# Fifteen small loads behind the last load of a weight stream, and a wait for each at the end

## The chip, the cores and the metric

One core of a Trainium2 chip runs the whole program. The metric is the device time of one execution in microseconds (us). A ratio is the mean time of one kernel's runs over the mean of the other's runs of the same rounds; it is therefore not quite the ratio of the medians quoted beside it. Its 95% interval is given in brackets. The span of a profile, from the first to the last instruction, is about 1.2 us shorter than the timed execution.

## The reference, cut to what matters

The reference is one decode step of a transformer block with modulation: attention of one token over a window of 1024 cached keys and values, then a gated feed-forward layer. Only its end matters here:

```
x = x + gb * ((gelu(h @ w_gate) * (h @ w_up)) @ w_down)     # w_down: 1536 x 640, bf16
return x                                                    # 2 x 1 x 640, bf16
```

## The kernel before

All large loads are issued on the SyncE queue (SP), in the order in which they are needed: `w_mod`, `wq`, the key and value tiles, `wo`, `w_gate`, `w_up`, and `w_down` in four pieces of 3, 5, 3 and 1 rows per partition. The kernel records its operations in a list; `S.dma` records a load with its own semaphore, a counter that instructions can wait for, and a finished load adds 16 to it: in the traces each DMA engine that carries a share of it sends its own update when it is done (here called an increment). SP, DVE, ACT and PE are the program's names for SyncE, VectorE, ScalarE and TensorE. The output's store is the last DMA on the same queue, and SP's last act is to wait for it.

```
WD_SPLIT = [(9, 3), (0, 5), (5, 3), (8, 1)]
...
wd_src = B_w_down.rearrange("(p r) n -> p (r n)", r=FC)
for ci, (r0, nr) in enumerate(WD_SPLIT):
    dst, src = wd_v[:, r0:r0 + nr, :].rearrange("p r n -> p (r n)"), wd_src[:, r0 * D:(r0 + nr) * D]
    S.dma("sp", k_dma(dst, src), sem_wd[ci], writes=[("wd", ci)], deps=r3_dead, name="ld_wd%d" % ci)
... (feed-forward layer; the matmuls "down" wait for one piece of w_down each)
S.op("dve", ... outR)                       # finb = gb * y + X
S.dma("sp", k_dma(out[:, 0, :].rearrange("b (i n) -> i b n", i=NR), finb[0:P:RB, :]),
      sem_out, reads=["finb"], name="st_out")
S.resolve()
S.emit("sp", nc.sync, tail=lambda e: e.wait_ge(sem_out, 16))
```

## Time and profile before

| | before |
|---|---|
| time, median of the first 3 runs | 188.83 us |
| span of the profile | 187.6 us |
| packets on SP's DMA queue | 6492, 76.88 MB |
| the last piece of `w_down` has landed (its 16th semaphore increment, in the trace) | 184.75 us |
| the output's store is issued | 185.87 us |
| the output has landed | 187.58 us |

The kernel is bound by its stream of loads. From the page of the kernel before, the busy tenths of the DMA engines in 40 slices of the span, SP's DMA queue (packets, MB, share of 16 engines' span) and the chain of work that ended last, by engine:

```profile
DMA  7999998999999999999999999999999999999991
...
q1 hardware_dynamic: 6492, 76.88, 97.1%
...
DMA 71%; DVE 15%; PE 7%; ACT 2%; SPq 2%; issue 1%
```

The DMA engines are nearly always busy until the last slice. Whatever is added costs time only if it delays this stream, or lengthens the short chain from the stream's end to the output's landing. That chain is in the timeline of the kernel before (start us, duration us, engine, line, operation, output<-input; in brackets how long the engine was idle and what released it):

```profile
184.79 0.10 PEld L684 LDWEIGHTS ps<-r,aT 128*17 128x17 bf16 x4 [0.20 <-DMA r<-in_B_w_down_dram]
185.16 0.33 DVE L689 TENSOR_TENSOR fin<-ps,modR 128x160 f32<-128x160 f32 x1 [2.75 <-PE ps L684]
185.52 0.32 DVE L691 TENSOR_TENSOR finb<-fin,X 128x160 bf16<-128x160 f32 x1
185.87 0.69 SPq L266 DMA_DIRECT2D out_dram<-finb  x1
```

The last four matmuls wait for the last piece, two DVE operations follow, and the store is issued 1.1 us after the piece has landed. The end is the store's own way, some 1.7 us. The timeline of SP in the kernel before (line 266 is the helper that issues every DMA) shows how much room SP has there:

```profile
150.35 0.43 SPq L266 DMA_DIRECT2D r<-in_B_w_gate_dram  x1
150.83 0.91 SPq L266 DMA_DIRECT2D r<-in_B_w_up_dram  x2
151.78 10.69 SPq L266 DMA_DIRECT2D r<-in_B_w_down_dram  x4
185.87 0.69 SPq L266 DMA_DIRECT2D out_dram<-finb  x1
```

An issue takes 0.43 us, but the four of `w_down` took 10.69 us together: the trace gives 0.43, 0.43, 2.02 and 7.68 us. SP was held up there; I take it that the queue had no room, which the trace doesn't say. SP then did nothing for 23.4 us, until the result was there. SP's waits, as the trace's list of waits gives them for the stretch from 150 us on (who waited for whom: us in total, times, longest):

```profile
SPq L266 <- DVE finb L691: 23.4, 1, 23.4
SPq L697 <- DMA out_dram<-finb: 1.0, 1, 1.0
```

### The profile page before, as it was taken

Reading aid. Unit: us, or ns where it says so; the run is one execution under the profiler, and the core shown is the slowest. Engines: PE = TensorE matmul, PEld = TensorE weight load, DVE = VectorE, ACT = ScalarE, POOL = GpSimd, SP = SyncE. Lnnn points to the kernel's source line nnn. Section 1 sums busy time; section 2 is a strip of 40 time slices with the busy share of each in tenths; the row PEclk is TensorE's granted clock in tenths of the full one; section 3 lists DMA queues with packets and bytes.
Section 4 is the critical chain, followed back from the end, with each engine's and each line's share of the span. In section 5 each row is a group of like instructions: output and inputs, shape, how many; then the busy total and the mean of one; then the engine's idle time right before and its main releaser. Section 6 shows DMA issues by size and latency. Waiting matters only on the chain.

```text
span 187.6 us, 2409 instructions
## 1 busy us (share of the span) xinstructions
PE 107.5 (57%) x1039; PEld 51.1 (27%) x1039; DVE 98.2 (52%) x147; ACT 29.9 (16%) x72; POOL 5.1 (3%) x23
## 2 busy tenths in 40 slices
PE   0014730742968887676676655675497395364462
PEld 0011200210323443333423323233253152353121
DVE  6131100019588988886595695775865933003211
ACT  3041100082001221112011110210120103103400
POOL 8200000000000000000000000000000000000000
PEclk9999999997587999999879999999969967569696
DMA  7999998999999999999999999999999999999991
GB/s 254 402 451 435 430 459 372 422 435 424 430 422 422 427 425 426 427 424 420 419 432 432 422 423 422 421 438 422 424 423 422 419 488 428 416 384 442 398 396 45
DMA packets 6518, 77.03 MB, mean 411 GB/s; under 512 B 746, under 2 KB 876, under 8 KB 1516
## 3 DMA queue, kind: packets, MB, share of 16 engines
q1 hardware_dynamic: 6492, 76.88, 97.1%
q8 instruction: 8, 0.13, 0.3%
q10 hardware_dynamic: 16, 0.01, 0.0%
q14 instruction: 2, 0.02, 0.0%
HBM read 76.88 MB, written 0.00 MB: 410 GB/s over the span
## 4 chain that ended last, share of the span: by engine, by line
DMA 71%; DVE 15%; PE 7%; ACT 2%; SPq 2%; issue 1%
DMA ring<-in_A_k_cache_dram 37%; DMA ring<-in_A_wq_dram 17%; DMA r<-in_B_w_down_dram 17%; DVE prod L490 9%; PE ps L502 4%; DVE S_sb L509 4%; PE ps L467 2%; SPq L266 2%; ACT qbc L483 2%; DVE ps L485 1%; DVE M L512 1%; ACT qrow L474 1%; PE ps L526 0%; DVE bcR L519 0%; PE ps L684 0%
## 5 line engine op out<-in xcount | busy, mean ns | idle before, releaser
L490 DVE TENSOR_TENSOR prod<-ring,qbc 128x3072 bf16<-128x3072 bf16 x32 | 55.9, 1751 | 14.3 <-DMA ring<-in_A_k_cache_dram 14.3
L502 PE MATMUL ps<-prod,ident_b 128*128 128x512 bf16 x192 | 52.9, 419 | 14.4 <-DVE prod L490 14.4
L502 PEld LDWEIGHTS ps<-prod,ident_b 128*128 128x128 bf16 x192 | 17.5, 104 | 40.2 <-DVE prod L490 17.5
L509 DVE TENSOR_REDUCE S_sb<-ps 128x32 f32<-128x1024 f32 x16 | 19.3, 1206 | 2.1 <-PE ps L502 2.1
L526 PE MATMUL ps<-bcR,bcL 5*128 5x4 f32 x32 | 6.1, 258 | 21.9 <-DVE bcR L519 21.9
L563 ACT ACTIVATE On<-ps,rden 128x384 bf16<-128x384 f32 x16 | 9.3, 580 | 43.5 <-DVE rden L561 21.1
L551 PE MATMUL ps<-ring,E_sb 128*8 128x384 bf16 x256 | 15.5, 369 | 0.0
L534 ACT ACTIVATE E_sb<-Sb_sb 128x128 bf16<-128x128 f32 x16 | 5.0, 310 | 56.4 <-DVE Sb_sb L531 56.4
L467 PE MATMUL ps<-ring,hT 128*2 128x512 bf16 x60 | 6.7, 626 | 9.8 <-DMA ring<-in_A_wq_dram 8.8
L526 PEld LDWEIGHTS ps<-bcR,bcL 5*128 5x128 f32 x32 | 4.7, 183 | 26.1 <-DVE bcR L519 26.1
L477 DVE CAST qrow<-ps 128x512 bf16<-128x512 f32 x1 | 0.7, 692 | 15.7 <-PE ps L467 15.7
L622 PE MATMUL ps<-ring,oT 128*17 128x160 bf16 x192 | 5.5, 294 | 5.6 <-DMA ring<-in_A_wo_dram 5.6
L531 DVE TENSOR_TENSOR Sb_sb<-S_sb,ps 128x128 f32<-128x128 f32 x16 | 4.6, 287 | 7.6 <-PE ps L526 7.6
L540 PEld LDWEIGHTS ps<-denp,maskc 128*128 128x128 f32 x32 | 7.1, 224 | 3.7 <-ACT E_sb L534 0.9
L641 DVE TENSOR_TENSOR lnt<-ps,modR 128x160 f32<-128x160 f32 x1 | 0.3, 325 | 12.6 <-PE ps L622 12.6
L445 PE MATMUL ps<-r,scT 128*17 128x480 bf16 x40 | 4.3, 597 | 3.9 <-DMA r<-in_w_mod_dram 3.9
L622 PEld LDWEIGHTS ps<-ring,oT 128*17 128x17 bf16 x192 | 4.9, 117 | 6.2 <-DMA ring<-in_A_wo_dram 6.2
L551 PEld LDWEIGHTS ps<-ring,E_sb 128*8 128x8 bf16 x256 | 5.1, 90 | 3.7 <-issue 1.2
L396 PE MATMUL ps<-st,selstat 128*128 128x2 f32 x4 | 0.9, 298 | 8.6 <-ACT sqj L392 8.6
L467 PEld LDWEIGHTS ps<-ring,hT 128*2 128x2 bf16 x60 | 1.7, 114 | 14.7 <-DMA ring<-in_A_wq_dram 9.7
L576 PE MATMUL ps<-On,zsel 128*128 128x96 bf16 x64 | 5.2, 241 | 0.7 <-ACT On L563 0.7
L540 PE MATMUL ps<-denp,maskc 128*128 128x1 f32 x32 | 5.1, 230 | 0.8 <-ACT E_sb L534 0.8
(81 smaller groups left out, 71.2 us busy)
## 6 DMA issues: line engine op xcount, KB each, us to landing
ring<-in_A_k_cache_dram SPq DMA_DIRECT2D x16, 1536.0 KB, 24.4
ring<-in_A_v_cache_dram SPq DMA_DIRECT2D x16, 1536.0 KB, 24.2
r<-in_w_mod_dram SPq DMA_DIRECT2D x1, 4800.0 KB, 14.3
ring<-in_A_wq_dram SPq DMA_DIRECT2D x1, 4608.0 KB, 32.3
ring<-in_A_wo_dram SPq DMA_DIRECT2D x1, 4480.0 KB, 23.4
ring<-in_A_wq_dram SPq DMA_DIRECT2D x1, 3072.0 KB, 21.2
ring<-in_A_wo_dram SPq DMA_DIRECT2D x1, 2720.0 KB, 24.1
r<-in_B_w_gate_dram SPq DMA_DIRECT2D x1, 1920.0 KB, 25.0
```

The source lines that it names most:

```text
L467: last = e.matmul(ps[32 * i:32 * i + B, n, :], lhsT=hT[:, k, :], rhs=wv[:, kk, i, n * QW:(n + 1) * QW], start=(k == 0), stop=(k == KT - 1) ...
L490: S.op("dve", lambda e: e.tensor_tensor(out=prod[:, 2 * (g % 2) + ci, :, :], in0=ring[:, sl, ci * JC * Dh:(ci + 1) * JC * Dh].rearrange("p ...
L502: last = e.matmul(o_ap, lhsT=ident_b[:, :], rhs=prod[:, pz, :, t * GC:(t + 1) * GC], start=(t == 0), stop=(t == NCH - 1))
L509: S.op("dve", lambda e: e.tensor_reduce(out=S_sb[:, z, :], in_=ps[:, 2 * z:2 * z + 2, :].rearrange("p k (j c) -> p (k j) c", c=GC), axis=A ...
L526: S.op("pe", lambda e: e.matmul(ps[:, BK_T, P:P + HQ], lhsT=bcL[:, :], rhs=bcR[:, z, :], start=True, stop=True), reads=[("bcR", z), "bcL"] ...
L531: S.op("dve", lambda e: e.tensor_tensor(out=Sb_sb[:, z, :, :], in0=S_sb[:, z, :].unsqueeze(2).broadcast_to([P, J, HQ]), in1=ps[:, BK_T, P: ...
L534: S.op("act", lambda e: e.activation(out=E_sb[:, z, :, :], in_=Sb_sb[:, z, :, :], func=ACTF.Exp, scale=SCALE, accum_out=denp[:, z:z + 1]), ...
L540: S.op("pe", lambda e: e.matmul(ps[:, BK_T, P + 16:P + 17], lhsT=maskc[:, :], rhs=denp[:, z:z + 1], start=True, stop=True), reads=[("denp" ...
L551: last = e.matmul(ps[32 * i:32 * i + 2 * HQ, BK_O, 0:ON], lhsT=E_sb[:, z, 2 * jp:2 * jp + 2, :].rearrange("p j h -> p (j h)"), rhs=ring[:, ...
L563: S.op("act", lambda e: e.activation(out=On[:, quad % 2, b, :], in_=ps[:, BK_O, 0:ON], func=ACTF.Identity, scale=rden[:, z:z + 1]), reads= ...
L576: last = e.matmul(ps[:, BK_OT, 0:B * NT].rearrange("p (b t) -> p b t", b=B), lhsT=zsel[:, jj, x:x + P], rhs=On[:, quad % 2, :, jj * Dh + d ...
L622: last = e.matmul(ps[32 * i:32 * i + RM, BK_M, 0:DR], lhsT=oT[:, t, :], rhs=wv[:, tl, i, :], start=(t == 0), stop=(t == NT - 1), tile_posi ...
```

## The change

It is a probe. Fifteen loads, of 1 to 15 rows with a different row length each so that their packets can be told apart in a trace, are put behind the last piece of the stream, and SP also waits for all of them at the end. Nothing uses the data. This is the whole diff, with its unchanged lines cut:

```diff
@@ -261,6 +261,8 @@
         sem_out = S.sem("d_out")
+        sem_probe = {k: S.sem("d_probe%d" % k) for k in range(1, 16)}
+        probe = sb("probe", [16, 15, 272], BF16)
@@ -637,6 +639,10 @@
             S.dma("sp", k_dma(dst, src), sem_wd[ci], writes=[("wd", ci)], deps=r3_dead, name="ld_wd%d" % ci)
 
+        for k in range(1, 16):
+            w = 32 + 16 * k
+            S.dma("sp", k_dma(probe[0:k, k - 1, 0:w], B_w_down[0:2 * k, :].rearrange("(p r) n -> p (r n)", r=2)[:, 0:w]), sem_probe[k],
+                  writes=[("probe", k)], name="ld_probe%d" % k)
@@ -694,7 +700,7 @@
-        S.emit("sp", nc.sync, tail=lambda e: e.wait_ge(sem_out, 16))
+        S.emit("sp", nc.sync, tail=lambda e: [e.wait_ge(s, 16) for s in [sem_out] + list(sem_probe.values())])
```

## The prediction

> **What bounds the kernel now.** The stream of loads: in the page's slices the DMA engines are 90% or more busy nearly to the end, at about 425 GB/s, and the chain of waits gives DMA 71% of the span (187.6 us; 188.83 timed). The end, from the timeline: the last piece of w_down, issued at 154.79 us, lands at about 184.75; four matmuls and two DVE operations end at 185.84; the output's store is issued on SP at 185.87 (0.69 us), its packets move at 187.15 to 187.25, and SP's final wait ends at 187.6. The 16 engines finish the last piece at different times, 182.9 to 184.75.
>
> **What the change adds.** It removes nothing. 15 loads (k rows of 64+32k bytes, 47 KB in all) enter SP's queue behind that last piece and ahead of the store, and 15 semaphore waits follow the final wait.
>
> 1. DMA time. In the trace a store row of 320 bytes takes 20 to 32 ns, a load row of 1280 bytes 55, a semaphore packet 9, with gaps of 6 to 40. The Trainium skill, "DMA: Bandwidth & Descriptors", section "Why a DMA increments its semaphore by 16 and not by 1", says that a DMA uses the largest number of engines up to 16 that divides the slowest dimension, the lowest-numbered ones. The trace agrees: the store (2 by 4 rows) left 8 data and 4 semaphore packets, the load of c 2 and 2. So load k uses k engines, one row each; the first engine gets 15 rows and 15 semaphore packets, about 0.6 us (estimate: 15 x (22+9+10 ns)). The queue's packets rise from 6492 by 240 to 6732. They stand behind the last piece, so don't delay it, and have moved by about 185 us, 2 us before the store's. No cost.
>
> 2. SP's issue. An issue costs 0.33 to 0.69 us, 15 cost 7 to 10; SP is free from 162.47 to 185.87 (23.4 us in the wait list). But the queue is nearly full: the last two loads' issues took 2.02 and 7.68 us, with about 8 loads of 9 packets per engine outstanding. If room is given by packets, the 30 small ones on the first engine fit in by about 180 us (estimate: 40 packets drained since 162.5): no cost. If by loads, whatever their size, the last six wait for the stream's end and the store goes 2 to 3 us late. I hold the first at 80%.
>
> 3. The tail. 15 more waits on SP, already satisfied, after the output has landed. One takes 17 ns, and SP's instructions follow each other after 40 to 60: 15 x 17 to 75 ns = 0.3 to 1.1 us, most likely 0.6 (estimate), in full on the critical path.
>
> **Prediction.** 188.83 + 0.6 = 189.4 us; with one chance in five of a late store, the range is 188.8 to 191.0. Chances: faster by over 2% 0.01, within 2% 0.94, slower by over 2% 0.05.
>
> **What would show each step.** The last piece lands again near 184.7 us; 6732 packets; the fifteenth small load's issue ends before 182 us, and the store is issued within 0.3 us of 185.9; 15 instructions after the output's landing take 0.3 to 1.1 us.
>
> **What would make it wrong.** Room counted by loads (store late); a stall at each small load's semaphore packet (none shows between loads now: 6 ns); small packets far over 55 ns on the first engines, which also carry the store; final waits far over 75 ns.

## The result and the profile after

| | before | after |
|---|---|---|
| time, median of 4 runs | 188.91 us | 189.09 us |
| ratio | 1 | 1.0008 [0.9995, 1.0021] |
| last piece of `w_down` landed | 184.75 us | 184.99 us |
| small loads: the last issue ends / the last increment lands | – | 175.74 / 186.75 us |
| store issued | 185.87 us | 186.12 us |
| output landed | 187.58 us | 187.85 us |
| last wait ends | 187.62 us | 187.87 us |

The time is the same within the interval. The profiled run of the changed kernel is 0.25 us longer, but that lies ahead of everything that was added: its issue of `w_gate`, before the first small load, is already 0.19 us later (150.54 against 150.35). From the last piece's landing to the end of the last wait, before took 2.87 us and after 2.88. Nothing was added there.

The lines of the page of the changed kernel that answer to those of before:

```profile
DMA  7999998999999999999999999999999999999991
...
q1 hardware_dynamic: 6732, 76.93, 97.1%
...
DMA 71%; DVE 16%; PE 6%; SPq 2%; ACT 2%; issue 1%
```

The queue has exactly 240 packets more, as predicted: 120 rows and 120 semaphore packets. In the trace the row lengths count out one by one: one packet of 96 bytes, two of 128, and so on to fifteen of 544. The end of the timeline of the changed kernel is the same chain as before (line numbers have moved by 2 to 6):

```profile
185.03 0.10 PEld L690 LDWEIGHTS ps<-r,aT 128*17 128x17 bf16 x4 [0.18 <-DMA r<-in_B_w_down_dram]
185.40 0.33 DVE L695 TENSOR_TENSOR fin<-ps,modR 128x160 f32<-128x160 f32 x1 [2.83 <-PE ps L690]
185.76 0.33 DVE L697 TENSOR_TENSOR finb<-fin,X 128x160 bf16<-128x160 f32 x1
186.12 0.67 SPq L268 DMA_DIRECT2D out_dram<-finb  x1
```

SP's timeline and SP's waits in the changed kernel show the fifteen issues, and that SP still waits 10.4 of its former 23.4 us for the result:

```profile
151.96 10.70 SPq L268 DMA_DIRECT2D r<-in_B_w_down_dram  x4
162.70 13.04 SPq L268 DMA_DIRECT2D probe<-in_B_w_down_dram  x15
186.12 0.67 SPq L268 DMA_DIRECT2D out_dram<-finb  x1
```

```profile
SPq L268 <- DVE finb L697: 10.4, 1, 10.4
SPq L703 <- DMA out_dram<-finb: 0.6, 1, 0.6
```

Two things in the trace were not as I had expected them.

First, the final waits. The program names the output's semaphore first. The compiled program has eight wait instructions, each for two semaphores, and they begin in the middle of the list and work outwards. The output's wait, at one end of the list, came last. These are SP's records in the trace of the changed kernel; semaphore 121 is the output's, 122 to 136 are the small loads':

```
start us   ns   waits for
186.840    28   129, 128
186.914    28   130, 127
186.987    28   131, 126
187.046    28   132, 125
187.108    28   133, 124
187.167    28   134, 123
187.228    28   135, 122
187.288   583   136, 121 (output)
```

The output's last increment is at 187.85 us. Seven of the eight waits ran while the output was still on its way.

Second, the small loads took far longer to land than to move. Their last packet of data begins at 184.61 us, but the last semaphore increment lands at 186.75 us. The increments of successive small loads come one after another. The trace doesn't name the engine of an increment, but the first engine's can be picked out from the load of one row, which has only one: 183.16, 183.34, 183.52, 183.70, 183.88, 184.07, 184.24 us for loads 1 to 7, that is one every 0.18 us. The latest increments of loads 6 to 15 run from 184.94 to 186.75 us, 0.20 us apart; by their times they belong to one engine, whose first small load was load 6. It isn't the engine that ended the stream last: its first of these increments, at 184.94, comes ahead of the last piece's last one at 184.99. The data packets of the same loads on that engine begin 20 to 29 ns apart, from 184.26 to 184.48 us. So its increment for load 15 landed 2.2 us after its semaphore packet had begun (184.50 us). So the small loads ended 1.1 us before the output landed, not the 2 us that I had counted with, and with more of them that could run out.

### The profile page after: what moved, and what is told of

Read it like the earlier page. It is cut to its first block, busy times and chain, and to the rows that moved or that the text cites. A ratio compares the mean times of both kernels' runs of the same rounds, so it can differ in the third digit from the quotient of the medians.

```text
span 187.9 us, 2430 instructions
## 1 busy us (share of the span) xinstructions
PE 105.6 (56%) x1038; PEld 51.3 (27%) x1039; DVE 98.1 (52%) x147; ACT 29.9 (16%) x72; POOL 5.1 (3%) x23
## 3 DMA queue, kind: packets, MB, share of 16 engines
q1 hardware_dynamic: 6732, 76.93, 97.1%
## 4 chain that ended last, share of the span: by engine, by line
DMA 71%; DVE 16%; PE 6%; SPq 2%; ACT 2%; issue 1%
DMA ring<-in_A_k_cache_dram 37%; DMA ring<-in_A_wq_dram 17%; DMA r<-in_B_w_down_dram 17%; DVE prod L492 10%; DVE S_sb L511 4%; PE ps L469 3%; PE ps L504 3%; SPq L268 2%; ACT qbc L485 2%; DVE ps L487 1%; DVE M L514 1%; PE ps L528 0%; PE ps L690 0%; DVE bcR L521 0%; DVE Sb_sb L533 0%
## 5 line engine op out<-in xcount | busy, mean ns | idle before, releaser
L504 PE MATMUL ps<-prod,ident_b 128*128 128x512 bf16 x192 | 50.5, 405 | 14.2 <-DVE prod L492 14.2
L553 PE MATMUL ps<-ring,E_sb 128*8 128x384 bf16 x256 | 14.8, 356 | 0.0
L624 PE MATMUL ps<-ring,oT 128*17 128x160 bf16 x192 | 6.4, 325 | 7.2 <-DMA ring<-in_A_wo_dram 7.2
L624 PEld LDWEIGHTS ps<-ring,oT 128*17 128x17 bf16 x192 | 5.8, 131 | 7.6 <-DMA ring<-in_A_wo_dram 7.6
L542 PEld LDWEIGHTS ps<-denp,maskc 128*128 128x128 f32 x32 | 6.6, 208 | 3.5 <-ACT E_sb L536 0.9
L578 PE MATMUL ps<-On,zsel 128*128 128x96 bf16 x64 | 4.6, 223 | 0.7 <-ACT On L565 0.7
```

Of the source, the lines that this page charges most:

```text
L504: last = e.matmul(o_ap, lhsT=ident_b[:, :], rhs=prod[:, pz, :, t * GC:(t + 1) * GC], start=(t == 0), stop=(t == NCH - 1))
L542: S.op("pe", lambda e: e.matmul(ps[:, BK_T, P + 16:P + 17], lhsT=maskc[:, :], rhs=denp[:, z:z + 1], start=True, stop=True), reads=[("denp" ...
L553: last = e.matmul(ps[32 * i:32 * i + 2 * HQ, BK_O, 0:ON], lhsT=E_sb[:, z, 2 * jp:2 * jp + 2, :].rearrange("p j h -> p (j h)"), rhs=ring[:, ...
L578: last = e.matmul(ps[:, BK_OT, 0:B * NT].rearrange("p (b t) -> p b t", b=B), lhsT=zsel[:, jj, x:x + P], rhs=On[:, quad % 2, :, jj * Dh + d ...
L624: last = e.matmul(ps[32 * i:32 * i + RM, BK_M, 0:DR], lhsT=oT[:, t, :], rhs=wv[:, tl, i, :], start=(t == 0), stop=(t == NT - 1), tile_posi ...
```

## The experiments

The theory is that the change is free for three reasons. SP's issues fit in its idle time. The loads stand behind the last piece, so they delay no data that anybody waits for. And both the small loads' increments and the waits for them end before the output has landed. The rivals are that it costs about 0.16 us, the difference of the medians; that it would be free wherever it stood; or, as I had predicted, that only the packets' 20 to 30 ns matter and not an increment every 0.18 us. (The 0.16 us is the figure put on record; the medians of the table above differ by 0.18.) All runs below gave correct results. Four kernels (the change again, the output's wait moved, the twenty-four loads, and the fifteen ahead of the last piece) ran on one chip with one set of runs of the kernel before; the two with one load and the one with 128 rows ran on another with theirs; the twelve loads ran on a third with their own.

### The change again

The kernel is unaltered.

> The changed kernel unaltered, as a control on this chip. Theory A (everything that was added ends before the output has landed): ratio to the kernel before 1.000 to 1.001; the 15 small loads are issued on SP between about 162.7 and 176 us; on one engine their semaphore increments land about 0.18 us apart; the last of them lands near 186.7 us, about 1 us before the output's last increment. Rival B (the change costs 0.16 us, as the medians of the first runs differ): ratio 1.001 with an interval that leaves out 1.

Measured: 189.06 us against 188.93, ratio 1.0005 [0.9992, 1.0018]. The small loads are issued from 162.33 to 176.10 us, the first engine's increments are 0.18 us apart, the last lands at 186.68 us, and the output at 188.06 us. Rival B's 0.16 us is not confirmed, as the interval has 1 in it, nor is it excluded. All five kernels here whose additions end before the output lands (the change twice, and three below) have ratios from 1.0005 to 1.0009. Each interval includes 1, but all five lie on one side, so some 0.1 us may be real. It isn't in the tail, where after the output's last increment both kernels end within 0.04 us, and one load shows it as much as fifteen. One candidate is that the last piece itself comes a little later: from the third piece's last increment to the last piece's it is 0.42 to 0.45 us in all seven kernels with loads behind the last piece, and 0.38 us in the one profile of the kernel before. One profile can't show that, so this stays open.

### The output's wait moved to the middle of the list

```diff
-        sem_out = S.sem("d_out")
-        sem_probe = {k: S.sem("d_probe%d" % k) for k in range(1, 16)}
+        sem_probe = {k: S.sem("d_probe%d" % k) for k in range(1, 9)}
+        sem_out = S.sem("d_out")
+        sem_probe.update({k: S.sem("d_probe%d" % k) for k in range(9, 16)})
...
-   tail=lambda e: [e.wait_ge(s, 16) for s in [sem_out] + list(sem_probe.values())]
+   tail=lambda e: [e.wait_ge(s, 16) for s in list(sem_probe.values())[0:8] + [sem_out] + list(sem_probe.values())[8:]]
```

> Same loads; only the place of the output's semaphore in the list of final waits is moved to the middle, so that the compiled program should wait for the output in the first of eight final wait instructions, not in the last. Theory A (the final waits were free only because the output's wait came last): seven wait instructions follow the output's landing at 60 to 75 ns each, span and time up by 0.4 to 0.5 us against the unaltered change (ratio to before about 1.003). Rival (waits on semaphores that are already there cost nothing in any order): no difference, ratio 1.001 or less. If the compiler orders the waits in another way, the trace will show it and the run tells nothing of the cost.

Measured: 189.55 us, ratio 1.0029 [1.0015, 1.0043]; the control beside it has 1.0005, so the new order costs about 0.0024 x 188.9 = 0.45 us; the six runs of each don't overlap (189.37 to 189.76 against 188.97 to 189.34). In the trace the output's last increment is at 187.81 us, the first of the eight waits starts at 187.825, the eighth ends at 188.301. The queries for the line of the final waits show the move of one line of code. Columns: count, then duration in ns (least, median, most), then first and last start. In the changed kernel:

```profile
L703 SPq EVENT_SEMAPHORE  x8: 28/28/583, 186.8 to 187.3; - x8
```

With the output's wait in the first pair:

```profile
L704 SPq EVENT_SEMAPHORE  x8: 28/28/28, 187.8 to 188.3; - x8
```

In the first, seven waits pass and the last is held for 583 ns. In the second, none shows a long duration: the first begins only when the output has landed, and the other seven follow with 0.06 to 0.07 us from start to start. So a wait that is already satisfied does have a cost. In the change it was hidden by the order of the waits in the compiled program. (The edit moved the output's semaphore in the list and in the order of creation, so the runs don't tell which of the two sets the order of the waits.)

### Twenty-four loads on all engines

```diff
-        probe = sb("probe", [16, 15, 272], BF16)
+        probe = sb("probe", [16, 24, 160], BF16)
-        for k in range(1, 16):
+        for k in range(1, 25):
-            S.dma("sp", k_dma(probe[0:k, k - 1, 0:w], B_w_down[0:2 * k, :]...[:, 0:w]), sem_probe[k], ...)
+            S.dma("sp", k_dma(probe[0:16, k - 1, 0:160], B_w_down[0:32, :]...[:, 0:160]), sem_probe[k], ...)
```

> 24 loads of 16 rows of 320 bytes in place of the 15, so each of the 16 engines carries 24 small rows and 24 semaphore packets. Theory A (an engine's semaphore increments of small loads land one after another, 0.18 us apart): on the engine that ends the stream last (185.0 us) the last increment lands at about 185.0 + 24 x 0.185 = 189.4 us, and the final wait, which needs it, ends 1.4 to 1.7 us later than before: ratio about 1.008. Rival B (what counts is the packets' 20 to 30 ns, as I predicted): the last lands by 186.5 us and the ratio is 1.000 to 1.002. SP's 24 issues should end by 182 us in both.

Measured: 190.89 us, ratio 1.0098 [1.0084, 1.0111]. SP's issues end at 181.25 us, so they are not the cause. The last piece of `w_down` lands at 184.83 us, as before. The last increment of the last small load lands at 189.39 us, where the theory had 189.4. The time rose by 1.85 us (0.0098 x 188.9), a little above the 1.4 to 1.7 us that the expectation gave. With each load's 16 increments sorted by time, the step per load from the first load's to the last's was 0.171 to 0.199 us at every rank, so each engine took about that per load; all engines did so at once, so this is a rate of each engine and not of something that they share. SP's waits in this kernel:

```profile
SPq L268 <- DVE finb L696: 4.6, 1, 4.6
...
SPq L702 <- DMA probe<-in_B_w_down_dram: 1.7, 9, 0.4
```

At the end SP now waits nine times for small loads. They also hold up the output itself: its four increments land at 187.57, 187.59, 188.36 and 188.66 us instead of within 0.05 us of each other. The two late ones presumably stood behind small loads' increments on their engines, which the trace doesn't name: the last small load has increments at 188.18 and 188.46 us, 0.18 and 0.19 us ahead of them.

### Twelve of them

The edit is the one above, with 12 in place of 24.

> 12 loads of 16 rows of 320 bytes behind the last piece, half of the 24. If the small loads cost only what their increments, 0.18 to 0.19 us apart on an engine, stick out beyond the output's landing (about 187.5 to 187.8 us), then 12 of them end at about 184.9 + 12 x 0.187 = 187.1 us on the engine that ends last, and cost nothing: ratio 0.999 to 1.002. If the cost were proportional to their number (half of the 1.98 us of the 24), ratio 1.005.

Measured: 188.97 us against 188.94, ratio 1.0007 [0.9994, 1.0021]. The last increment lands at 187.15 us, the output at 187.68 us. Half the loads cost nothing, not half. What counts is how far the row of increments sticks out beyond the output's landing.

### The fifteen loads ahead of the last piece

```diff
         for ci, (r0, nr) in enumerate(WD_SPLIT):
+            if ci == len(WD_SPLIT) - 1:
+                for k in range(1, 16):
+                    ... the same 15 loads ...
             dst, src = wd_v[:, r0:r0 + nr, :]...
             S.dma("sp", k_dma(dst, src), sem_wd[ci], ...)
-        for k in range(1, 16):
-            ... the 15 loads ...
```

> The same 15 loads, issued just ahead of the last piece of w_down instead of behind it. Theory A (the semaphore increments of an engine land in order, 0.18 us apart): the last piece's increment on the engine that is last stands behind the small loads' increments (10 on that engine), so the last piece lands at 186.4 to 186.8 us instead of 184.75 to 185.0, and the time rises by 1.5 to 2.0 us: ratio 1.008 to 1.011. Rival B (only the packets' time counts, about 10 x 35 ns on that engine): the last piece lands 0.3 to 0.4 us later, ratio 1.002. Rival C (order does not matter, the change is free anywhere): ratio 1.000.

Measured: 190.50 us, ratio 1.0081 [1.0068, 1.0094], that is 1.5 us more. The third piece of `w_down`, ahead of the small loads, lands at 184.39 us (184.37 before); the last piece, behind them, at 186.35 us. The timeline of this kernel shows the last four matmuls held back:

```profile
184.44 0.58 PE L691 MATMUL ps<-r,aT 128*17 128x160 bf16 x12 [0.50 <-DMA r<-in_B_w_down_dram]
186.39 0.10 PEld L691 LDWEIGHTS ps<-r,aT 128*17 128x17 bf16 x4 [1.71 <-DMA r<-in_B_w_down_dram]
...
187.47 0.67 SPq L268 DMA_DIRECT2D out_dram<-finb  x1
```

By the packets, the last piece was hardly late: its last packet begins at 184.61 us, against 184.28 before. Its last packet moved 0.3 us later, but its last increment landed 1.6 us later. Its later issue is not the cause: that ended at 173.08 us, 9 us before its first packet began. The increments show the queue: of the fifteen of the last small load, fourteen are followed by one of the last piece 0.17 to 0.21 us later. So on the engines that carried small loads the last piece's increment stood behind theirs. Packets tell when an engine worked, not when anybody may use the data. The Trainium skill, "DMA: Bandwidth & Descriptors", section "Queues, rings and completion order", says that the increment is a strongly ordered write which lands only after every earlier write from that engine. This trace agrees, and adds the rate.

### One load instead of fifteen, behind the last piece

```diff
-        for k in range(1, 16): ... 15 loads ...
+        S.dma("sp", k_dma(probe[0:15, :, :], B_w_down[0:225, 0:160].rearrange("(p r) n -> p r n", r=15)), sem_probe[1],
+              writes=[("probe", 1)], name="ld_probe")
```

It has 225 rows of 320 bytes and 15 semaphore packets, together the same 240 packets as the fifteen.

> One load of 15 x 15 rows of 320 bytes (15 rows on each of 15 engines, one semaphore packet each) in place of the 15 loads. Theory S (the 0.18 us belongs to each semaphore increment, that is to each load): its last increment lands about 0.4 to 0.7 us after the last piece's, near 185.5 us, instead of 186.7. Rival R (it belongs to each small row): 15 x 0.18 us, near 187.5 us. The time is that of before in both (ratio 0.999 to 1.002), as it ends before the output lands.

Measured: 189.12 us against 188.97, ratio 1.0006 [0.9994, 1.0019]. The load's last increment lands at 185.08 us, 0.25 us after the last piece's 184.83. That is even less than theory S expected, and far from rival R's 187.5. So the 0.18 us belongs to each load on an engine, not to each small row. Every load here ends in one increment on each of its engines, so no run tells the cost of the increment from another cost of each load.

### That one load ahead of the last piece

The edit is the one above, in the place of the experiment before it.

> That one load of 15 x 15 rows, issued ahead of the last piece of w_down, to be held against the 15 loads there (ratio 1.0081, last piece landing at 186.35 us). Theory S: one semaphore and 15 rows of 20 to 30 ns on an engine stand ahead of the last piece: it lands 0.3 to 0.5 us later than in the kernel before, 185.1 to 185.4 us; ratio 1.001 to 1.003. Rival R: 15 x 0.18 us later, 187.4 us; ratio 1.014.

Measured: 189.56 us against 188.97, ratio 1.0030 [1.0018, 1.0043], 0.57 us more. The last piece lands at 185.49 us, just outside the expected 185.1 to 185.4. The cleaner figure is from the third piece's last increment to the last piece's: 0.38 us before, 0.43 in the change, 0.61 here and 1.96 with the fifteen loads. In this one profile the third piece, which stands ahead of the small load, also came later than in the others of its rounds (184.87 us against 184.25 and 184.38), so not all of the 0.7 us by which the last piece is later than before (184.75 us) is the small load's. With the same number of packets and more bytes, one load costs about a third of what fifteen cost in that place. Rival R is out.

### Fifteen loads of 128 rows

```diff
-        probe = sb("probe", [16, 15, 272], BF16)
+        probe = sb("probe", [P, 15, 32], BF16)
-            S.dma("sp", k_dma(probe[0:k, k - 1, 0:w], ...), sem_probe[k], ...)
+            S.dma("sp", k_dma(probe[:, k - 1, :], B_w_down[0:P, 0:32]), sem_probe[k], ...)
```

> 15 loads of 128 rows of 64 bytes behind the last piece: each takes 9 packets on every engine (8 rows and the semaphore), 135 per engine in all instead of at most 30. Theory P (room in the queue is given by packets): the issues drag on to the end of the stream, the fifteenth ends after 185.5 us (about 187 to 188.5), the output's store is issued 1.5 to 3 us late, time up by 1.5 to 3 us, ratio 1.008 to 1.016. Rival L (room is given by loads, whatever their size): the fifteenth is issued near 176 us as in the change, store on time; ratio at most 1.003. The increments on one engine also tell the semaphore's cost from the row's: theory S (0.18 us for each semaphore) expects 0.18 to 0.4 us from one load's increment to the next, rival R (0.18 us for each small row) about 1.6 us.

Measured: 189.13 us against 188.97, ratio 1.0009 [0.9996, 1.0023]. The fifteen issues end at 185.74 us, 10 us later than in the change. The timeline ends:

```profile
183.14 2.60 SPq L268 DMA_DIRECT2D probe<-in_B_w_down_dram  x3
...
185.45 0.33 DVE L696 TENSOR_TENSOR finb<-fin,X 128x160 bf16<-128x160 f32 x1
185.81 0.70 SPq L268 DMA_DIRECT2D out_dram<-finb  x1
```

Theory P has the right direction: the issue depends on the packets of a load and not on the number of loads, so rival L, with 176 us, is out. But its size was wrong. The fifteenth was through just in time and the store was not late, so the slowing by 1.5 to 3 us that I expected did not come. Nor do I know the rule by which the queue gives room: the first small load's issue took 4.29 us here, with 9 packets on each engine, 4.29 us with 2 in the twenty-four, and 4.38 us with 16 in the one load. That is not a wait for as many places as the load needs. The increments on an engine came 0.17 to 0.25 us apart, with 8 rows to each: theory S again. The last of them landed at 187.54 us and the output at 187.55, so this kernel stood at the very edge.

## Why the prediction was right or wrong

The time, 189.09 us, is 0.3 us below the 189.4 predicted, inside the range and in the likeliest class. Part of that is luck: the range began at the old time of 188.8, so no cost at all also fell inside it. The 0.6 us that the sum added did not come: the time rose by 0.15 us (0.0008 x 188.9) with an interval that includes zero, and none of that was in the tail, where the prediction had put it. Point by point:

- **The bound, right.** The stream keeps its shape; the last piece lands at 184.99 us, as the wait for it in the timeline confirms. In the control's profile, its slowest run, it landed at 185.21 us; between 184.68 and 185.02 in the five others with loads behind it.
- **Step 1, DMA time: right in that it costs nothing, wrong in when it ends.** The 6732 packets are exact, and the rows had moved by 184.64 us, as I said ("by about 185 us"). But I took the end of the packets for the end of the loads. I named "a stall at each small load's semaphore packet" as a way to be wrong and dismissed it because packets follow each other after 6 ns. They do (the next begins 6 ns after the semaphore packet began); the increments land 0.18 us apart all the same. The margin before the output's landing was 1.1 us. Twenty-four loads on all engines used it up and cost 1.9 us (0.0098 x 188.9); twelve did not; and in front of the last piece the same fifteen loads cost 1.5 us. What made the change free is thus its place in the queue and its small number, not that it was cheap; the margin itself was not foreseen.
- **Step 2, SP's issue: right, with the time mis-sized.** The store was not held up. The fifteenth issue ended at 175.74 us, earlier than the 180 us estimated. Room does not go by loads: the loads of 128 rows were issued 10 us later than those of 1 to 15. So the late store that I gave one chance in five was no risk here. The exact rule stays open.
- **Step 3, the tail: wrong.** "15 more waits on SP, already satisfied, after the output has landed ... 0.3 to 1.1 us, most likely 0.6 (estimate), in full on the critical path" failed. The unit cost was about right: with the output's wait in the first pair, seven paired waits cost 0.45 us by the times and 0.45 us in the trace. The place was wrong. I read the order of the waits from the source; the compiled program has them in pairs with the output's last, so they ran while the output was in flight, and the measured cost is nothing beyond noise. This is the term that made 189.4 out of 188.8.

## What to carry to other kernels

Here, small loads behind the last needed load of a queue were free within the noise as long as their semaphore increments, one every 0.18 to 0.2 us for each load on an engine, ended before the output's landing; the same loads ahead of a needed one delayed that one's landing though the packets hardly showed it. So judge a load by its last increment and not by its packets, and make one load of many rows rather than many loads where something waits behind them. Before costing a list of waits, look at the order and pairing in which the compiled program has them: wait instructions that were already satisfied (here of two semaphores each) cost 0.06 to 0.07 us each, but only where they came after the one that counted.

## What the Trainium skill lacked or had wrong

- "DMA: Bandwidth & Descriptors", section "Anatomy of one DMA — SWDGE (gpsimd) path", calls the write of the semaphore "essentially free". For loads issued from SP the packets agree (9 ns, and the next packet begins 6 ns after it began), but the page lacks the rate at which increments land: small loads' increments on one engine were 0.171 to 0.199 us apart in the run of twenty-four, where all 16 engines were at it, and 0.18 to 0.20 us in the change, where only some were.
- The same page, section "Queues, rings and completion order", gives the order of increments but not its consequence in time: fifteen small loads moved the landing of the needed load behind them by 1.6 us in the profile, while its last packet began only 0.3 us later.
- The same page, section "Rules for kernel authors", advises to coalesce small transfers and speaks of overhead; the runs put a number on it for a place ahead of a needed load: 1.5 us for fifteen loads, 0.57 us for one load with as many packets.
- The same page, section "Why a DMA increments its semaphore by 16 and not by 1", has the rule for the number of engines right: loads of 1 to 15 rows left 1 to 15 data packets and as many semaphore packets (6732 in all), and one early update is in the trace 0.1 to 0.2 us after each issue ends.
- I found on no page how much SP can issue ahead before it is held up. Here a load's issue took 0.43 us with room, and 2.0 to 7.7 us with about eight loads of 9 packets per engine outstanding; more packets held it up longer (fifteen loads were through at 175.7 us with 1 to 15 rows, at 185.7 with 128 rows).
- I found on no page that consecutive waits are compiled in pairs and in another order than they are written in: eight instructions for 16 waits, the first-named in the last pair, 0.45 us at stake.
